# A fused recurrent-attention and MLP kernel: the opening fifth of its instruction order rewritten, with the first alpha and k loads in front of the first weight slice

## The chip, the cores and the metric

The kernel runs on one core of one Trainium2 chip. The core has five engines, each with its own queue of instructions that it works off strictly in order: PE (the matrix engine, with its weight loads shown apart as PEld), DVE (vector), ACT (scalar/activation), POOL (general purpose) and SP, which here only issues DMA transfers. Engines wait for each other through semaphores. Sixteen DMA engines move data between DRAM and the on-chip memory SBUF; matrix products land in a second memory, PSUM. The metric is the time of one execution in microseconds (us) on the device, as a median of several runs.

## The reference

Two blocks, one behind the other. The first is gated linear attention as a recurrence over 768 tokens, for 4 batches, 8 heads and head size 48, all in float32:

```
state = alpha[t][:, None] * state + outer(k[t], v[t])
y[t]  = q[t] @ state
```

The result, 3072 tokens by 384 features, goes into a two-layer MLP with hard-swish: `h = x @ w_in` (384 to 2048), `g = h * clip(h + 3, 0, 6) / 6`, `out = g @ w_out` (2048 to 384). The two weights come as float64 and are turned into float32 on the chip, by integer operations on their two 32-bit words.

## The kernel before, in words

**Tiling.** The sequence is cut into 24 chunks of 128 tokens (6 for each batch); two chunks make a group of 256 tokens for the MLP, so there are 12 groups. The recurrence of a chunk is done in a closed form: running products of alpha scale k and q, a masked product of the two gives the scores, and a 48x48 state is carried from chunk to chunk (in half chunks of 64 tokens). Groups 0 and 1 use the plain first product of the MLP (six matrix products for a pair of hidden blocks); from group 2 on it uses a scheme with fewer products and more sums, whose sums of weights (25 of them) and of activations DVE makes. The second product has a scheme of the same kind from group 1 on.

**The order of the work** is written out by hand as one list of about 1,790 words in one call of `run` (from line 753). Nothing rearranges it: each word calls one function of the table `steps` (line 730), which issues its instructions at once, and so each engine's queue holds its instructions in the order of the words. A word is the step's name, then its numbers: `la.1` is "load alpha of chunk 1", `f.0.6.3` "first product, group 0, part 6, into PSUM bank m3".

The steps that matter here, with their engines and lines:

- `la`, `lk`, `lq` (SP, line 256): alpha, k, q of one chunk, 192 KB in pieces of 192 bytes; `lv` (line 274): v, in two DMAs of 96 KB. `w` (lines 162, 166): one of 16 weight slices of 768 KB, eight of w_in, then eight of w_out.
- `d2`, `d1`, `dx` (ACT, lines 196, 186, 191), `d3` (DVE, lines 203 and 205, or 207, 208 and 210) and `d4` (POOL, line 217): the conversion of one weight slice. `d4` ends it, and frees the slice's load buffer.
- `ta`, `tk`, `tq` (PE, line 284): transposes into one of four PSUM banks t0 to t3; `ca` (ACT, line 302) copies alpha out. From chunk 6 on these are transposes on DVE (line 288).
- `r` (DVE, lines 311 and 315) and `p` (line 322): the running products; `k` and `q` (line 334): scaling k and q. `kb` (PE, line 376) and `ck` (ACT, line 380): k turned back.
- `u` (PE, line 431), `sm` (DVE, lines 439 and 441), `st` (POOL, line 411), `sv` (ACT, line 421, POOL, line 417): the state. `sc` (PE, line 348), `m` (DVE, line 358), `qa` (ACT, line 368), `ya`, `yb` (PE, line 457), `cy` (ACT, line 466): scores, mask, attention output, and its copy as the MLP's input.
- `fa`, `fb` (PE, line 491) and `f` (line 480): first MLP product by half groups and whole groups, into banks m0 to m3; `fr` (ACT, line 496) and `fg` (DVE, line 500): hard-swish. `b` (PE, line 518): second product of group 0. `P` (PE, line 705), `s`, `x`, `G` (DVE, lines 649, 666, 721): second product with sums. `M` (PE, line 602), `y`, `xc` (DVE, lines 539 to 543): first product with sums.
- `z.m.n` (PE, line 534): n products of the identity with itself, whose result nobody reads. There are 26 of them in the opening. One shows as two instructions in the profile. `pd` (POOL, line 251): six small memsets of the buffers for chunks 6 and up.

**What binds the loads.** All DMAs are issued by SP, in order, and their completion semaphores are used in turn, eight of them: the n-th DMA waits until the one eight before it has landed.

Of the kernel before, what the change touches and what calls it, by code (L numbers as in the profile page):

```python
# [17 lines left out]
def kernel(  # L18
# [42 lines left out]
    G = 2  # L61
# [512 lines left out]
    for i in range(8):  # L574
        r, o = divmod(i, 3)
        spots.append(raws[r].rearrange("p n w -> p (n w)").bitcast(FP)[:, o * QB : (o + 1) * QB])
    xc = consts.tile([C, len(X_SUMS), C], FP, tag="xc")
# [174 lines left out]
    with tc.manual_schedule():  # L752
        run("""z.0.5 z.0.3 z.0.1 qa.0.0 w.0 d2.0 d3.0 la.0 ta.0.0 z.0.8 lk.0 tk.0.1 la.1 ta.1.2
               lq.0 tq.0.3 lk.1 lv.0.0 d1.0 ca.0 r.0 p.0 k.0 kb.0.0 z.0.2 z.0.2 q.0 la.2 dx.0 ca.1
               r.1 ck.0 u.0.2.1 sm.0.0 qa.0.1 sv.0.1 tk.1.0 p.1 sc.0.2.3 w.2 lq.1 sm.0.1 k.1 m.0
               ta.2.0 z.0.2 d1.2 ca.2 d2.2 kb.1.0 ck.1 r.2 tq.1.2 q.1 dx.2 lv.1.1 u.1.3.1 z.0.3
               lq.2 w.1 lk.2 d4.0 lk.3 la.3 la.4 w.3 lq.3 lv.2.2 lk.4 w.5 pd.0 sv.0.0 pd.1 st.1
               sm.1.0 p.2 d3.2 sm.1.1 ya.0.3 yb.0 sc.1.0.2 m.1 d4.2 sv.1.1 cy.0 qa.1.1 sv.1.0 d1.1
               st.2 d2.1 dx.1 fa.0.1 tq.2.1 q.2 tk.2.3 k.2 fa.2.0 sc.2.0.2 d3.1 m.2 d4.1 ta.3.1
               ta.4.3 kb.2.0 qa.1.0 ca.3 r.3 ca.4 r.4 ya.1.2 yb.1 tk.3.1 fa.1.2 p.3 k.3 qa.2.1  # L760
               qa.2.0 cy.1 d2.3 d3.3 fb.2 fb.1 tq.3.1 q.3 sv.2.0 d1.3 ck.2 u.2.3.2 sm.2.0 d4.3
               fr.0.2.0 tk.4.0 d2.5 sv.2.1 k.4 sm.2.1 st.3 fg.0.2 d3.5 w.6 lv.3.0 lq.4 w.7 fb.0
               sc.3.1.3 m.3 kb.3.2 kb.4.0 f.0.3.3 ya.2.1 ck.3 d1.5 d4.5 d1.6 d2.6 d3.6 d4.6 sv.3.0
               qa.3.1 fr.0.1.0 fr.0.3.1 la.5 w.4 yb.2 u.3.3.2 sm.3.0 fg.0.3 fg.0.1 sm.3.1 f.0.5.0
               tq.4.3 f.0.6.3 ta.5.2 cy.2 ck.4 d2.7 qa.3.0 d1.7 d3.7 d4.7 fr.0.5.1 fr.0.0.0 sv.3.1
               fg.0.0 fg.0.5 p.4 d2.4 ya.3.0 yb.3 cy.3 fr.0.6.1 w.9 d2.9 ca.5 d1.9 d1.4 dx.4 la.6
               w.8 d3.4 lk.5 w.10 d3.9 ca.6 q.4 fg.0.6 d4.9 w.12 lq.5 lv.4.1 d2.8 f.0.7.2 st.4
               f.1.1.1 f.1.7.0 sc.4.0.2 f.1.3.3 qa.4.0 d1.8 fr.0.7.0 r.6 d3.8 d4.8 d4.4 w.11 fg.0.7
               m.4 fr.1.1.0 fr.1.7.1 fg.1.7 fg.1.1 d2.10 d1.10 f.1.0.2 d2.12 d3.10 r.5 d4.10 w.13
               fr.1.0.0 fr.1.3.1 fg.1.3 fg.1.0 d3.12 lq.6 f.1.6.0 f.1.2.1 u.4.1.0 tk.5.3 sm.4.0  # L770
               sv.4.0 d1.12 qa.4.1 d4.12 w.15 fa.4.3 fr.1.2.0 fr.1.6.1 d2.11 d2.13 f.1.4.2 d1.11
               sm.4.1 lv.5.0 lk.6 fg.1.2 k.5 kb.5.1 tq.5.3 d3.11 p.5 d4.11 tq.6 fg.1.6 q.5 p.6
               d3.13 d1.13 d4.13 tk.6 st.5 w.14 la.7 lk.7 ck.5 sv.4.1 b.0.0.1 ya.4.2 yb.4 sc.5.0.3
               m.5 cy.4 d2.15 fr.1.4.1 fg.1.4 d3.15 d2.14 d3.14 u.5.2 b.0.1 f.1.5.0 fb.4 b.1.0.2
               b.1.1 qa.5.0 fr.1.5.1 fg.1.5 d1.14 fr.0.4.0 d1.15 qa.5.1 d4.14 d4.15 sm.5.0 fg.0.4
               ca.7 sv.5.1 sv.5.0 ya.5.3 tk.7 s.1.0.0 x.0 k.6 x.1 y.6 y.1 yb.5 P.1.1.3 b.1.2 cy.5
               b.1.3 kb.6.0 P.1.0.0 b.0.2 lv.6.2 y.3 y.5 y.9 xc.2.1 y.2 s.1.1.1 y.7 s.1.3.2 x.2
               s.1.2.3 y.8 y.4 y.0 q.6 bo.1 K.1.0 G.1.0.0 P.1.2 K.1.1 s.1.4 xc.2.3 y.10 r.7 xc.2.4
               P.1.3.3 K.1.2 ck.6 P.1.4 b.0.3 xc.2.5 y.15 y.11 y.12 x.3 G.1.1.1 s.1.5 y.13 y.16 k.7
               P.1.5 u.6.3.0 sc.6.1.2 P.1.6 y.14 y.17 y.19 xc.2.6 sm.6.0 G.1.2.2 y.20 xc.2.0  # L780
               M.2.0.2 lv.12.1 la.8 O.1.1 O.1.0 ca.8 y.18 y.21 y.23 so.1 G.1.3.3 n.2.0.8 bo.0 lq.7
               lv.7.0 O.1.2 m.6 xc.2.2 xc.2.10 xc.2.7 tq.7 r.8 p.7 xc.2.8 sv.6.1 M.2.15.3 M.2.1
               kb.7.3 n.2.1.9 M.2.16 M.2.2 n.2.2.10 qa.6.1 M.2.7.0 n.2.7.11 sm.6.1 xc.2.9 q.7 p.8
               M.2.3 M.2.4 n.2.4.12 M.2.8 o.2.0.0 M.2.5 n.2.5.13 qa.7.0 st.7 sv.6.0 lk.8 O.1.3 lq.8
               lk.9 la.9 la.10 tk.8 tq.8 lq.10 lq.9 ya.6.1 yb.6 M.2.9 z.1.3 M.2.18.1 o.2.1.0
               e.2.1.1 M.2.10 cy.6 ck.7 sc.7.0.2 u.7.1.3 n.2.10.14 M.2.11 qa.7.1 ca.9 la.11 y.22
               M.2.6.2 h.2.1 q.8 m.7 e.2.0.0 h.2.0 n.2.11.15 qa.6.0 n.2.18.10 qa.8.1 M.2.12 M.2.19
               n.2.12.12 M.2.13 sm.7.0 sv.7.1 r.9 k.8 o.2.3.0 sv.7.0 ya.7.0 y.24 o.2.5.0 n.2.13.12
               o.2.2.0 yb.7 cy.7 sc.8.1.2 xc.3.1 o.2.2.1 e.2.2.1 xc.3.3 o.2.3.1 M.2.14 xc.3.4
               xc.3.0 xc.3.5 o.2.4.0 xc.3.7 xc.3.6 o.2.6.0 P.2.0.1 M.3.0.2 M.2.17 h.2.2 o.2.6.1  # L790
               e.2.3.0 h.2.3 o.2.7.0 K.2.0 n.3.0.12 M.3.1 n.3.1.9 e.2.5.1 M.3.7.0 n.3.7.13 xc.3.8
               o.2.7.1 xc.3.2 kt.8 e.2.6.0 h.2.6 tk.9 M.3.2 n.3.2.10 e.2.4.0 P.2.1.3 h.2.4 h.2.5
               s.2.0.14 e.2.7.0 G.2.0.1 h.2.7 M.3.3 M.3.4 n.3.4.8 k.9 s.2.1.11 M.3.8 o.3.0.0 ca.10
               kt.9 P.2.3.3 s.2.2.15 s.2.3.14 lv.8.2 kw.8 kr.8 lk.10 sm.7.1 xc.3.9 M.3.5 n.3.5.11
               K.2.2 e.3.0.1 xc.3.10 M.3.9 o.3.1.0 P.2.2 K.2.1 u.8.0.3 M.3.18.2 s.2.5 M.3.10
               n.3.10.14 n.3.18.15 e.3.1.0 s.2.4 P.2.4 tq.9 h.3.0 st.8 sv.8.0 M.3.11 n.3.11.8 tk.10
               p.9 sm.8.0 q.9 r.10 k.10 qa.9.0 qa.9.1 m.8 sm.8.1 h.3.1 M.3.19 o.3.5.0 kt.10 P.2.5
               G.2.2.0 st.9 M.3.12 sc.9.0.1 qa.8.0 n.3.12.10 o.3.3.0 kw.9 lv.9.0 kr.9 sv.8.1
               u.9.2.3 sm.9.0 sv.9.1 sv.9.0 G.2.1.2 sm.9.1 st.10 M.3.15.2 M.3.16 M.3.6.3 M.3.13 m.9
               o.3.4.0 o.3.6.0 tq.10 n.3.13.10 o.3.2.0 e.3.4.1 ya.8.2 yb.8 ya.9.3 yb.9 cy.9 M.3.14  # L800
               M.3.17 cy.8 xc.4.1 P.2.6 e.3.5.0 G.2.3.3 o.3.2.1 xc.4.3 h.3.4 xc.4.4 o.3.6.1 xc.4.5
               xc.4.0 xc.4.6 e.3.2.1 M.4.0.0 n.4.0.10 P.3.0.1 xc.4.7 o.3.7.0 p.10 h.3.5 o.3.3.1
               xc.4.8 M.4.7.3 M.4.1 xc.4.2 h.3.2 o.3.7.1 lk.11 O.2.2 tk.11 e.3.6.0 e.3.3.1 h.3.3
               P.3.1.2 e.3.7.1 n.4.1.13 M.4.2 K.3.0 ca.11 q.10 h.3.6 r.11 k.11 h.3.7 n.4.7.15
               lv.10.2 lv.11.0 kw.10 sc.10.0.1 kr.10 G.3.0.0 u.10.3.2 sm.10.0 qa.10.1 n.4.2.14
               M.4.3 M.4.4 M.4.8 s.3.0.9 xc.4.9 s.3.2.12 s.3.1.11 P.3.3.2 n.4.4.8 M.4.5 o.4.0.0
               e.4.0.0 sv.10.1 sm.10.1 xc.4.10 kt.11 O.2.0 O.2.3 lq.11 m.10 s.3.3.9 s.3.5 M.4.9
               o.4.1.0 P.3.2 sv.10.0 st.11 n.4.5.11 K.3.2 la.13 M.4.18.0 p.11 tq.11 lk.12 tk.12
               K.3.1 M.4.10 n.4.10.9 q.11 qa.10.0 n.4.18.12 e.4.1.1 la.12 s.3.4 ca.12 h.4.0 r.12
               P.3.5 G.3.2.1 h.4.1 M.4.11 P.3.4 n.4.11.8 M.4.12 n.4.12.14 qa.11.0 M.4.19 p.12  # L810
               G.3.1.3 lq.12 kw.11 O.2.1 tq.12 kr.11 u.11.3 sc.11.0.2 sv.11.0 O.3.1 lk.13 P.3.6
# [125 lines left out]
```

## Time and profile before

| | |
|---|---|
| median of 3 runs | 531.67 us (531.34 to 532.08) |
| the profiled execution's own time | 531.87 us |
| its span, first to last instruction | 530.1 us |
| PE busy | 520.6 us (98%) |
| DVE busy | 474.8 us (90%) |
| ACT busy | 257.5 us (49%) |
| POOL busy | 49.9 us (9%) |
| moved by DMA | 54.40 MB, of it 44.50 MB read from DRAM |

The profile comes from one execution. Its page gives the busy time of each engine, a picture of the span in 40 slices of 13.25 us, the chain of work that ended last, and groups of instructions by line. The trace behind it answers for any stretch: which instruction ran when, for how long, how long its engine sat idle before it and what released it; and, for a DMA, the time from its issue to its landing. Times in what follows count from the first instruction of the span. Consecutive instructions on an engine overlap a little, so a queue is added up by starts, not by durations.

### The profile page before, as it was taken

What the parts mean: (1) busy time and instruction counts of PE and PEld (TensorE: products, weight loads), DVE (VectorE), ACT (ScalarE), POOL (GpSimd) and SP (SyncE); (2) the same over time, 40 slices, a digit from 0 to 9 for tenths busy, and PEclk for the clock granted to TensorE, in tenths of its full rate; (3) what the DMA queues carried; (4) which work ended last, traced back from release to release, by engine and by line L of the source; (5) the groups of instructions that cost most, each with busy time, mean ns of one, the idle gap of its engine ahead of it and who ended that gap; (6) DMA issues with size and microseconds to landing.
All of it is one profiled execution on the core that took longest, in us unless ns stands there. A gap on an engine that the chain in (4) does not pass through costs nothing.

```text
span 530.1 us, 15131 instructions
## 1 busy us (share of the span) xinstructions
PE 520.6 (98%) x6306; PEld 495.8 (94%) x6306; DVE 474.8 (90%) x849; ACT 257.5 (49%) x503; POOL 49.9 (9%) x71
## 2 busy tenths in 40 slices
PE   7899999999999999999999999999999999999997
PEld 6688887789999999999999999999999999999997
DVE  7999999999999999998999999999999899595382
ACT  5789866003753644452644435642634544553340
POOL 7323343000000000000010000000000000000000
PEclk9999999999999999999999999999999999999999
DMA  9998877016515155254354456144464042100001
GB/s 171 218 251 247 246 208 171 1 37 157 123 29 124 29 125 125 59 138 104 81 112 112 96 122 139 24 116 106 112 142 102 16 92 56 44 2 2 15 16 37
DMA packets 124100, 54.40 MB, mean 103 GB/s; under 512 B 83328, under 2 KB 116864, under 8 KB 124032
## 3 DMA queue, kind: packets, MB, share of 16 engines
q1 hardware_dynamic: 124032, 53.44, 44.1%
q8 instruction: 49, 0.80, 0.7%
q14 instruction: 19, 0.16, 0.1%
HBM read 44.50 MB, written 8.91 MB: 101 GB/s over the span
## 4 chain that ended last, share of the span: by engine, by line
PE 92%; DMA 2%; DVE 2%; ACT 2%; POOL 0%; issue 0%; SPq 0%
PE m_ps L705 38%; PE m_ps L602 35%; PE m_ps L480 5%; PE t_ps L457 4%; PE m_ps L518 4%; PE t_ps L348 2%; PE t_ps L431 2%; DMA v<-in_v_dram 1%; DMA rings<-in_alpha_dram 1%; ACT raw L191 1%; DVE R L311 1%; PE m_ps L491 1%; PE t_ps L284 0%; POOL w L217 0%; PE m_ps L534 0%
## 5 line engine op out<-in xcount | busy, mean ns | idle before, releaser
L608 ACT COPY g_sb<-m_ps 128x512 f32<-128x512 f32 x110 | 63.5, 583 | 122.3 <-PE m_ps L602 101.7
L705 PE MATMUL m_ps<-w,g_sb 128*128 128x192 f32 x704 | 121.8, 327 | 0.0
L705 PEld LDWEIGHTS m_ps<-w,g_sb 128*128 128x128 f32 x704 | 113.7, 190 | 0.5
L705 PE MATMUL m_ps<-rings,g_sb 128*128 128x192 f32 x528 | 91.5, 326 | 0.0
L705 PEld LDWEIGHTS m_ps<-rings,g_sb 128*128 128x128 f32 x528 | 85.4, 190 | 0.4
L602 PE MATMUL m_ps<-xc,w 128*128 128x128 f32 x640 | 82.7, 277 | 0.0
L602 PEld LDWEIGHTS m_ps<-xc,w 128*128 128x128 f32 x640 | 77.5, 192 | 1.0
L496 ACT ACTIVATE r<-g_sb,half 128x512 f32<-128x512 f32 x80 | 56.8, 722 | 32.7 <-DVE g_sb L500 11.9
L500 DVE SCALAR_TENSOR_TENSOR g_sb<-r,g_sb 128x512 f32<-128x512 f32 x80 | 53.5, 680 | 4.5 <-ACT r L496 4.1
L602 PE MATMUL m_ps<-xT,raw 128*128 128x128 f32 x400 | 52.5, 277 | 0.0
L602 PEld LDWEIGHTS m_ps<-xT,raw 128*128 128x128 f32 x400 | 48.6, 192 | 0.6
L411 POOL TENSOR_TENSOR st<-sm,R 128x192 f32<-128x192 f32 x20 | 12.7, 635 | 340.6 <-DVE sm L441 293.8
L649 DVE TENSOR_TENSOR g_sb<-g_sb 128x512 f32<-128x512 f32 (+1 forms) x55 | 42.0, 792 | 0.2
L602 PE MATMUL m_ps<-xT,w 128*128 128x128 f32 x320 | 42.0, 276 | 0.0
L602 PEld LDWEIGHTS m_ps<-xT,w 128*128 128x128 f32 x320 | 39.3, 192 | 0.1
L368 ACT COPY A<-q 48x256 f32<-48x256 f32 x88 | 35.5, 403 | 5.1 <-DVE q L334 3.8
L358 DVE TENSOR_TENSOR A<-t_ps,mask 64x256 f32<-64x256 f32 x96 | 36.1, 414 | 0.4
L480 PE MATMUL m_ps<-xT,w 128*128 128x256 f32 x144 | 32.5, 381 | 0.0
L602 PE MATMUL m_ps<-xc,raw 128*128 128x128 f32 x240 | 31.8, 276 | 0.0
L311 DVE TENSOR_TENSOR_SCAN R<-t,ones 128x516 f32<-128x516 f32 x24 | 29.9, 1246 | 0.9 <-ACT t L302 0.8
L480 PEld LDWEIGHTS m_ps<-xT,w 128*128 128x128 f32 x144 | 26.9, 190 | 3.8
L602 PEld LDWEIGHTS m_ps<-xc,raw 128*128 128x128 f32 x240 | 29.6, 192 | 0.1
(104 smaller groups left out, 718.2 us busy)
## 6 DMA issues: line engine op xcount, KB each, us to landing
raw<-in_moe_w_out_dram SPq DMA_DIRECT2D x8, 768.0 KB, 5.1
raw<-in_moe_w_in_dram SPq DMA_DIRECT2D x6, 768.0 KB, 6.7
v<-in_v_dram SPq DMA_DIRECT2D x48, 96.0 KB, 3.2
out_dram<-oh SPq DMA_DIRECT2D x44, 96.0 KB, 1.7
far<-kq SPq DMA_DIRECT2D x64, 64.0 KB, 2.2
kb<-far SPq DMA_DIRECT2D x64, 64.0 KB, 2.1
aq<-in_alpha_dram SPq DMA_DIRECT2D x36, 96.0 KB, 2.5
qq<-in_q_dram SPq DMA_DIRECT2D x36, 96.0 KB, 2.6
```

Of the source, the lines that this page charges most:

```text
L311: nc.vector.tensor_tensor_scan(out=reverse(R, n - 1, n), data0=reverse(ax, n, n), data1=reverse(ones, n, n), initial=0.0, op0=ALU.mult, op ...
L358: nc.vector.tensor_tensor(out=to[:, a], in0=sc[a][half], in1=mask[half, half].unsqueeze(1).to_broadcast([HB, NP, HB]), op=ALU.mult)
L368: nc.scalar.copy(out=to[:, a], in_=Q_t[j][64 * a : 64 * a + D, :, half])
L457: nc.tensor.matmul(y_of(j, (i + 1) // 2, p)[:, HB * b : HB * b + HB], vb[:, p, e : e + 32], A_t[j][:, b, 2 * p + a], start=(b == 0 and i = ...
L480: nc.tensor.matmul(h[:, f], w1[:, kk, o : o + C], xT_t[g][:, kk], start=(kk == 0), stop=(kk == KT - 1))
L496: nc.scalar.activation(out=to, in_=h, func=AF.Relu, bias=half, scale=1.0 / 6.0)
L500: nc.vector.scalar_tensor_tensor(out=to, in0=r, scalar=1.0, in1=h, op0=ALU.min, op1=ALU.mult)
L518: nc.tensor.matmul(o_t[c], gs[0][:, f, c * C : (c + 1) * C], w2[:, f], start=(f == 0), stop=(f == NF - 1))
L602: nc.tensor.matmul(acc[g][i][:, f * C : (f + 1) * C], spots[w][:, f * C : (f + 1) * C], x_of(g, x), start=(first and f == 0), stop=last, s ...
L608: nc.scalar.copy(out=slots[z], in_=acc[g][i])
L649: nc.vector.tensor_tensor(out=out, in0=in0, in1=in1, op=ALU.subtract)
L705: nc.tensor.matmul(to[g], a, rhs[:, f], start=(first and f == 0), stop=(last and f == HF - 1), skip_group_check=True)
```

## The change

The same 1,790 words, in another order. They differ up to word 435; from there to the end the two lists are identical. By the profile's clock that is about the first 135 us. No step is added, removed or altered.

- SP: w slice 0 was the first transfer, in front of alpha 0, k 0, alpha 1, q 0, k 1. Now alpha 0, k 0, alpha 1 go first, then w slice 0, then k 1, q 0. Further on, v 1 moves in front of q 1; the loads of chunks 3 and 4 and slice 3 go as a3, w3, v2, a4, k4, k3, q3 (before: k3, a3, a4, w3, q3, v2, k4).
- DVE: `d3.0` goes from the front of the queue to behind `r.1`; `p` behind `k` for chunk 0; `q.1` from in front of `sm.1.0` to behind `sm.1.1`. Further on most `r`, `p`, `q`, `fg` and `d3` change places with neighbours.
- ACT: `d2.0` and `d1.0` go behind the copies of alpha 0 and 1.
- PE: alpha 0, k 0, alpha 1 are transposed right behind each other; eight of the idle products stand behind these three; two stand in front of `u.0`, and the two behind `ta.2` are gone from there. `ta.4` stands behind `yb.1`, `fb.1` behind `kb.3`, chunk 3's attention in front of chunk 2's, `sc.4` in front of `f.0.7`, `P.1.0` in front of `P.1.1`.
- POOL: `pd.0` and `pd.1` go from behind `d4.0` to behind `d4.7` and `d4.8`.
- Behind `xc.2.0`: `tk.7`, `ca.7`, `r.7`, `k.7` and `y.14` go from in front of `M.2.0` to behind it.

```
-        run("""z.0.5 z.0.3 z.0.1 qa.0.0 w.0 d2.0 d3.0 la.0 ta.0.0 z.0.8 lk.0 tk.0.1 la.1 ta.1.2
-               lq.0 tq.0.3 lk.1 lv.0.0 d1.0 ca.0 r.0 p.0 k.0 kb.0.0 z.0.2 z.0.2 q.0 la.2 dx.0 ca.1
-               r.1 ck.0 u.0.2.1 sm.0.0 qa.0.1 sv.0.1 tk.1.0 p.1 sc.0.2.3 w.2 lq.1 sm.0.1 k.1 m.0
-               ta.2.0 z.0.2 d1.2 ca.2 d2.2 kb.1.0 ck.1 r.2 tq.1.2 q.1 dx.2 lv.1.1 u.1.3.1 z.0.3
-               lq.2 w.1 lk.2 d4.0 lk.3 la.3 la.4 w.3 lq.3 lv.2.2 lk.4 w.5 pd.0 sv.0.0 pd.1 st.1
-               sm.1.0 p.2 d3.2 sm.1.1 ya.0.3 yb.0 sc.1.0.2 m.1 d4.2 sv.1.1 cy.0 qa.1.1 sv.1.0 d1.1
-               st.2 d2.1 dx.1 fa.0.1 tq.2.1 q.2 tk.2.3 k.2 fa.2.0 sc.2.0.2 d3.1 m.2 d4.1 ta.3.1
-               ta.4.3 kb.2.0 qa.1.0 ca.3 r.3 ca.4 r.4 ya.1.2 yb.1 tk.3.1 fa.1.2 p.3 k.3 qa.2.1
...
-               P.1.5 u.6.3.0 sc.6.1.2 P.1.6 y.14 y.17 y.19 xc.2.6 sm.6.0 G.1.2.2 y.20 xc.2.0
-               M.2.0.2 lv.12.1 la.8 O.1.1 O.1.0 ca.8 y.18 y.21 y.23 so.1 G.1.3.3 n.2.0.8 bo.0 lq.7
-               lv.7.0 O.1.2 m.6 xc.2.2 xc.2.10 xc.2.7 tq.7 r.8 p.7 xc.2.8 sv.6.1 M.2.15.3 M.2.1
...
+        run("""z.0.5 z.0.3 qa.0.0 la.0 z.0.1 ta.0.0 lk.0 la.1 w.0 tk.0.1 ta.1.2 z.0.8 lk.1 lq.0
+               ca.0 r.0 z.0.2 ca.1 d2.0 k.0 p.0 r.1 d3.0 kb.0.0 z.0.2 tq.0.3 q.0 ck.0 d1.0 dx.0
+               tk.1.0 p.1 lv.0.0 la.2 qa.0.1 w.2 z.0.2 u.0.2.1 sm.0.0 sv.0.1 k.1 sc.0.2.3 sm.0.1
+               m.0 ta.2.0 ca.2 d1.2 r.2 kb.1.0 ck.1 d2.2 lv.1.1 lq.1 u.1.3.1 z.0.3 tq.1.2 lq.2 w.1
+               lk.2 la.3 w.3 lv.2.2 la.4 lk.4 lk.3 lq.3 d4.0 w.5 sv.0.0 st.1 sm.1.0 d3.2 sm.1.1 q.1
+               p.2 ya.0.3 yb.0 sc.1.0.2 m.1 tq.2.1 q.2 dx.2 sv.1.0 cy.0 st.2 d4.2 sv.1.1 d1.1 d2.1
+               dx.1 qa.1.0 fa.0.1 tk.2.3 k.2 d3.1 d4.1 ta.3.1 sc.2.0.2 fa.2.0 m.2 kb.2.0 ca.3
+               qa.1.1 r.3 ya.1.2 yb.1 ta.4.3 fa.1.2 d2.3 d3.3 d1.3 cy.1 fb.2 ca.4 ck.2 qa.2.0
+               sv.2.0 r.4 d4.3 qa.2.1 fr.0.2.0 d2.5 w.6 lv.3.0 lq.4 w.7 u.2.3.2 tk.3.1 fb.0 sm.2.0
+               k.3 p.3 tq.3.1 tk.4.0 sm.2.1 st.3 fg.0.2 q.3 d3.5 f.0.3.3 sc.3.1.3 kb.3.2 fb.1 m.3
...
+               fr.0.5.1 ta.5.2 f.0.6.3 ya.3.0 yb.3 ya.2.1 yb.2 w.9 la.6 w.8 p.4 d3.7 d4.7 pd.0
+               fg.0.5 lk.5 w.10 q.4 fg.0.1 ca.5 d2.4 cy.3 fr.0.6.1 cy.2 d2.9 d1.4 d1.9 fr.0.0.0
+               d3.4 d3.9 fg.0.0 sc.4.0.2 f.0.7.2 f.1.7.0 f.1.1.1 dx.4 fr.0.7.0 d2.8 st.4 d4.9 w.12
...
+               y.17 y.12 y.19 x.3 y.20 G.1.1.1 xc.2.6 P.1.6 G.1.2.2 xc.2.0 tk.7 M.2.0.2 O.1.1 O.1.0
+               ca.8 ca.7 y.18 y.21 sm.6.0 r.7 y.23 so.1 G.1.3.3 n.2.0.8 bo.0 lq.7 lv.7.0 O.1.2 m.6
+               xc.2.2 k.7 xc.2.10 xc.2.7 tq.7 y.14 r.8 p.7 xc.2.8 sv.6.1 M.2.15.3 M.2.1 kb.7.3
```

## The prediction, made before the changed kernel was run

> **What bounds the kernel now.** I read the page first (busy shares, the 40 slices):
>
> ```profile
> PE 520.6 (98%) x6306; PEld 495.8 (94%) x6306; DVE 474.8 (90%) x849; ACT 257.5 (49%) x503; POOL 49.9 (9%) x71
> PE   7899999999999999999999999999999999999997
> DVE  7999999999999999998999999999999899595382
> ...
> ```
>
> PE is the bound, and only its first slices have holes. The table by stretches sizes them (after the length: busy time of PE, PEld, DVE, ACT, POOL):
>
> ```profile
> 0.00:13.25 13.25, 9.66 (x70) 8.89 (x74) 9.54 (x18) 6.92 (x9) 9.38 (x24) 1.00 1.13 171
> 13.25:26.50 13.25, 10.71 (x247) 9.23 (x247) 12.21 (x25) 10.11 (x18) 4.62 (x13) 1.00 1.06 218
> 26.50:39.75 13.25, 12.98 (x246) 11.89 (x246) 12.68 (x21) 11.20 (x20) 3.83 (x3) 1.00 1.08 251
> 39.75:53.00 13.25, 12.96 (x212) 11.03 (x211) 12.46 (x21) 13.02 (x24) 4.39 (x3) 1.00 0.87 247
> 53.00:132.00 79.00, 79.00 (x690) 65.89 (x689) 76.97 (x126) 36.04 (x63) 15.98 (x11) 1.00 0.53 136
> 132.00:530.00 398.00, 395.24 (x4857) 388.92 (x4855) 350.94 (x643) 180.18 (x373) 11.69 (x18) 1.00 0.35 80
> ```
>
> PE idles 3.59 + 2.54 + 0.27 + 0.29 = 6.7 us before 53 us, nothing from there to 132, and 2.8 behind that, where the word list is unchanged. PE's work is the same before and after, the 26 idle products included, so **the time changes by the change in PE's idle time up to 135 us**. From 53 to 132 DVE too is busy for 97%. What PE waits for, from the list of its waits up to 45 us (total, times, longest):
>
> ```profile
> PE m_ps L534 <- POOL ident masks.py:199: 1.5, 1, 1.5
> PE t_ps L284 <- DMA rings<-in_alpha_dram: 1.3, 1, 1.3
> PE t_ps L284 <- DVE k L334: 1.3, 1, 1.3
> PE t_ps L376 <- ACT t L302: 0.8, 1, 0.8
> PE t_ps L376 <- DVE k L334: 0.5, 1, 0.5
> ```
>
> The 1.5 stays: every engine starts with it. The next is alpha 0; the rest comes through DVE's chain. The timeline of the start (start, duration, idle before and its end in brackets):
>
> ```profile
> 1.46 4.18 PE L534 MATMUL m_ps<-ident 128*128 128x128 f32 x18 [1.46 <-POOL ident masks.py:199]
> 5.67 0.91 ACT L196 ACTIVATE w<-raw 128x768 f32<-128x768 f32 x1 [3.65 <-DMA raw<-in_moe_w_in_dram]
> 6.61 0.93 DVE L203 TENSOR_SCALAR w<-w 128x768 f32<-128x768 f32 x1 [2.43 <-ACT w L196]
> 6.96 0.63 PE L284 MATMUL t_ps<-ident,rings 128*128 128x128 f32 x4 [1.31 <-DMA rings<-in_alpha_dram]
> 7.42 1.95 PE L534 MATMUL m_ps<-ident 128*128 128x128 f32 x16
> 7.57 0.69 DVE L205 TENSOR_SCALAR w<-w 128x768 uint32<-128x768 uint32 x1
> 8.24 1.23 DVE L311 TENSOR_TENSOR_SCAN R<-t,ones 128x516 f32<-128x516 f32 x1
> 16.05 1.52 DVE L358 TENSOR_TENSOR A<-t_ps,mask 64x256 f32<-64x256 f32 x4
> 18.03 1.23 DVE L311 TENSOR_TENSOR_SCAN R<-t,ones 128x516 f32<-128x516 f32 x1 [0.47 <-ACT t L302]
> ```
>
> Two things matter. Nine idle products (18 instructions) hold PE until 5.64, so alpha is no use earlier. And DVE does `d3.0` from 6.61 to 8.24, while alpha 0 is still on its way: before, this work cost the chain nothing.
>
> **Loads.** Before, the landings were: w0 5.65, alpha 0 6.82, k 0 8.03, then one load of 192 KB each 1.2 us (q 0 10.44, k 1 11.65). With three loads in front, w0 lands near 5.65 + 3 x 1.2 = 9.25. Its 768 KB take about 2.1 us at the 386 GB/s of the best early stretch, so alpha 0, k 0, alpha 1 land near 4.7, 5.9, 7.1, q 0 at 11.65, k 1 at 10.4; the eighth DMA ends as before. Bounds for alpha 0: 4.4 (w0's landing less one load) and 6.8 (no gain). I take 4.7, the row it is nearest to being w0 in that place. The other moved transfers keep bytes and pace: v 1 comes about 1.2 earlier (it goes past q 1), q 1 as much later, slice 3 about 2.5 earlier, k 3 from 25 to near 32, where `tk.3` now stands at 33.7.
>
> **DVE's chain**, by starts. `ta.0` 5.66 instead of 6.96 and `ca.0` behind it (8.24 - 6.96 = 1.28 from transpose to `r.0`): `r.0` 6.95, **a gain of 1.29**. Then `r.0` 1.46, `k.0` 0.6, `p.0` 1.15, `r.1` 1.46 bring DVE to 11.6, and now `d3.0` stands there: 1.39 by the same pair at 22.00 (0.93 + 0.69 in the rows above, beside POOL's memsets). Its inputs are there: w0 9.25, `d2.0` 0.91 on ACT. So **the gain is spent again**: `q.0` 13.0, `p.1` 13.6 (0.3 slower, since `d4.0` now runs on POOL beside it, as `r.1` took 1.63 instead of 1.23 beside POOL), `sm.0.0` 15.05, `k.1` 15.6, `m.0` 16.2 against 16.05.
>
> What follows gains a little. `dx.0` and `qa.0.1` fill ACT before alpha 2's copy is due, so `ca.2` runs at 16.4 instead of 17.43 and the wait of 0.47 in front of `r.2` goes: `r.2` 17.7 (18.03). `u.1` has v 1 and `ck.1` at 18.5 (19.43 and 19.91), and `sm.1.0` no longer waits 0.38. Then `d3.2`, `sm.1.1`, `q.1` 21.15, `p.2`, `m.1` 22.9 (23.57), `q.2`, `k.2`, `d3.1` 25.6 (26.32), `m.2` 26.95 (27.73). DVE is 0.8 ahead; by `d3.6`, whose predecessors are then the same set, about 1.2 (44.2 against 45.4).
>
> **PE's idle time** on that chain: 1.46 at the start; 0.4 between k 0 and alpha 1; 0.8 before `tq.0` (q 0 is later); 1.2 before `ta.2` (it takes the bank from `k.1`; before 1.26); 0.6 before `kb.1` (0.77); 1.0 before `u.1`, since the two idle products behind `ta.2` moved forward; 0.3 each before `sc.1` and `sc.2`; 0.55 before `kb.2` (m.2's bank; 0.27). Sum 6.6. Before, up to there: 6.4, and 0.3 at 42.66. At the end of `yb.1` PE is at 29.75 against 30.65, with one transpose (`ta.4`, 0.55) less done: 0.35 ahead; if `ya.2`'s 0.29 at 42.66 goes too, **0.64 ahead**. Some of it I give back: `ta.4` arrives as alpha 4 lands (near 29.8).
>
> **From 40 to 135 us** PE can only keep or lose this. I added up DVE's and PE's words in both orders, from the times of before. Then `u.3` behind `m.3`, `kb.4` behind `k.4`, `sc.4` behind `q.4` and `f.0.7` behind `fg.0.1` come 0.2 to 0.4 too early for DVE (before, slacks of 0.7 to 4.4), which DVE's lead of 1.2 covers over PE's lead of 0.6. Later the least slacks are 0.6 (`P.1.5` behind `s.1.5`; before 1.0) and about 0.4 (`kb.7` behind `k.7`, now behind `y.23`; before over 5), while `M.2.0` gains 5 us of slack from the 4.7 us of DVE work put behind it. So 0.2 of waits, bounded by 0 and 1. POOL's memsets (12 x 0.33) leave 12.6 to 15.4, where DVE is slowed beside them, for a stretch in which POOL is idle for over 70%: nothing. `d4.0` to 15.5 is hidden: `fa.0` needs it at 23. ACT's table load moves with its first instruction, 1.28 in an idle 3.65: nothing.
>
> **Sum**: -0.64 + 0.2 = -0.4 on an execution of 531.87 (span 530.1, 1.8 around it), which lies 0.2 above its median of 531.67: **531.3 us**, a change too small to tell from none (I call 0.2%, 1.06 us, the limit of that).
>
> **Rivals.** (1) *Within 0.2%*, as above: chance 0.38, its own range 530.6 to 532.7.
> (2) *Slower: alpha 0 comes late.* Small pieces open the queue, and the first transfer starts on a cold DMA path; no row shows alpha in that place. Every 0.1 us behind 5.6 delays `r.0` by 0.1, and `d3.0` still stands on the chain. At the bound 6.8 DVE is 1.2 later all along: PE +1.2 - 0.4, and the four tight places of 40 to 52 lose their cover (+0.4): +1.2, 532.9. It decides from about 6.5 on, or with as much delay at w0 (past 10.7, `d3.0` waits). The rows speak for the arithmetic, the pace of 1.2 against so late a landing. With the tight places failing for another reason, 0.24.
> (3) *Slower: PE's clock falls back.* The first 18 instructions took 4.18/18 = 232 ns each, the next 16 1.95/16 = 122, all at a granted clock shown as 1.00. In the new order PE does only eight transposes between 14.7 and 18.5, 3.8 us; before, the longest such stretch was 9.4 to 12.1. If PE dropped to the slow rate for another 4.2 us there, `u.1` to `sc.1` (0.57 + 0.75 + 0.6 + 1.1 + 0.7 = 3.7) would double, less 0.6 of idle time: +3.1 - 0.4, 534.4; half of that if it recovers sooner. Chance 0.06. The Trainium skill says in "TensorE: Matmul & The Clock Gate", Part 1, that an idle window of about 3.4 us halves the clock, and in Part 4 that transposes don't count as busy; by these the stretch could just hold such a window. This trace has the slow start (232 ns) but no such fall.
> (4) *Faster by over 0.2%.* PE still waits 5 us between 6 and 29 in my chain. If `p.1` isn't slowed beside POOL (0.3), `d3.0` costs the least a half slice shows (1.36), transfers land 0.5 earlier with the shorter queue in front (0.8 before `tq.0`, 0.4 before `ta.1`), and the later waits vanish: -0.4 - 0.3 - 0.5 - 0.2 = -1.4, 530.3. Chance 0.32.
>
> The range goes to 529.4 below (all the waits of (4) half gone) and 533.6 above (half of (3), all of (2)). Faster 0.32, same 0.38, slower 0.30.
>
> **What would show it.** Right: alpha 0's transposes at 5.7, `r.0` near 7.0, `d3.0` between 11 and 13.5, `m.0` within 0.4 of 16.05, PE's idle time up to 53 us of 6 to 6.8, none from 53 to 132. Wrong: PE waiting for DVE past 40 us (lines 348, 376, 480), alpha 0 landing past 5.7, idle products or `u.1` at double duration near 19 us, or idle time below 5.6.

## The result: slower by 0.4%, and by how long the clock stayed low

The changed kernel takes 534.45 us in the median of 22 executions (531.06 to 536.43), the kernel before beside it 531.64 us (531.26 to 534.09): a ratio of 1.0041, 95% interval 1.0025 to 1.0057. The prediction was 531.3 us, range 529.4 to 533.6; the median lies 0.85 us above that range.

The 22 times do not lie around one value, and without this they can't be understood: executions of one kernel differ in the TensorE clock that was granted. In three the mean clock was 1.00, and they took 531.11 to 531.13 us. In three it was 0.997: 531.06 to 531.21. In the other sixteen it was 0.990 to 0.994, and these took 533.24 to 536.43. So the forecast sum came true where the clock held (531.12, some 0.5 us under the kernel before), and in most executions something else was paid on top: 2 to 5 us.

The profile of the changed kernel shows an execution whose clock held (531.11 us). Its page, busy shares and the first rows of the 40 slices:

```profile
PE 519.5 (98%) x6306; PEld 495.7 (94%) x6306; DVE 475.2 (90%) x849; ACT 258.1 (49%) x503; POOL 52.7 (10%) x71
PE   7799999999999999999999999999999999999997
...
PEclk9999999999999999999999999999999999999999
```

Its table by stretches (length, then busy time of PE, PEld, DVE, ACT, POOL, and the granted clock):

```profile
0.00:13.25 13.25, 10.58 (x102) 9.94 (x102) 9.65 (x20) 6.99 (x8) 6.64 (x20) 1.00 1.05 188
13.25:26.50 13.25, 9.86 (x240) 8.41 (x241) 12.73 (x25) 11.78 (x19) 6.78 (x5) 1.00 1.16 249
26.50:39.75 13.25, 12.92 (x209) 11.57 (x209) 12.85 (x22) 10.53 (x21) 4.80 (x4) 1.00 0.95 207
39.75:53.00 13.25, 12.63 (x248) 11.12 (x248) 12.49 (x21) 13.09 (x24) 6.00 (x10) 1.00 0.95 284
53.00:132.00 79.00, 79.00 (x665) 66.47 (x664) 77.28 (x126) 35.76 (x63) 18.18 (x18) 1.00 0.50 129
```

PE's idle time is 2.67 + 3.39 + 0.33 + 0.62 = 7.0 us up to 53 us, and none from there to 132. Before, it was 6.7, and 7.1 in a second profile of the kernel before (before_again, below), so the sum has hardly moved. But it lies elsewhere: the first stretch lost 0.9 of it, the second gained 0.85. What PE waits for there, by the list of its waits up to 30 us (total, times, longest):

```profile
PE m_ps L534 <- POOL ident masks.py:199: 1.5, 1, 1.5
PE t_ps L348 <- DVE s L439: 1.5, 1, 1.5
PE t_ps L284 <- DMA rings<-in_q_dram: 0.9, 1, 0.9
PE t_ps L431 <- ACT kb L380: 0.8, 1, 0.8
PE t_ps L376 <- ACT t L302: 0.7, 1, 0.7
```

The wait for alpha 0 (1.3) and that for `k.1` in front of `ta.2` (1.3) have gone. New is the second line: `sc.0` waits for DVE's copy in `sm.0.0`. The timeline of that place, first before the change, then after it:

```profile
13.13 0.57 PE L431 MATMUL t_ps<-v,kb 64*48 64x48 f32 x32
13.64 0.66 PE L284 MATMUL t_ps<-ident,rings 128*128 128x128 f32 x4
13.81 0.33 DVE L439 COPY s<-t_ps 128x192 f32<-128x192 f32 x1
14.06 1.22 DVE L322 TENSOR_TENSOR_SCAN P<-t 128x516 f32<-128x516 f32 x1
14.22 0.69 PE L348 MATMUL t_ps<-q,k 48*64 48x64 f32 x32
```

```profile
12.40 0.57 PE L431 MATMUL t_ps<-v,kb 64*48 64x48 f32 x32
...
12.91 1.23 DVE L322 TENSOR_TENSOR_SCAN P<-t 128x516 f32<-128x516 f32 x1
...
13.06 2.72 POOL L217 TENSOR_TENSOR w<-w,raw 128x768 int32<-128x768 int32 x1 [6.05 <-ACT raw L191]
14.06 0.33 DVE L439 COPY s<-t_ps 128x192 f32<-128x192 f32 x1
...
14.44 0.69 PE L348 MATMUL t_ps<-q,k 48*64 48x64 f32 x32 [1.47 <-DVE s L439]
```

`u.0` (L431) and `sc.0` (L348) both use bank t2 (`u.0.2.1`, `sc.0.2.3`), so the scores can't start before DVE has copied the state out of it. The change put `p.1` (L322) in front of that copy on DVE; before, it stood behind, and PE had the transposes of `tk.1` (L284, at 13.64) to do in the meantime, so `sc.0` followed without a wait. Beside it POOL's `d4.0` (L217) starts only 0.15 us after `p.1`.

### The profile page after: what moved, and what is told of

It is laid out like the page before. It is cut to its first block, busy times and chain, and to the rows that moved or that the text cites. A ratio compares the mean times of both kernels' runs of the same rounds, so it can differ in the third digit from the quotient of the medians.

```text
span 529.3 us, 15133 instructions
## 1 busy us (share of the span) xinstructions
PE 519.5 (98%) x6306; PEld 495.7 (94%) x6306; DVE 475.2 (90%) x849; ACT 258.1 (49%) x503; POOL 52.7 (10%) x71
## 4 chain that ended last, share of the span: by engine, by line
PE 93%; DVE 3%; DMA 2%; SPq 1%; ACT 1%; issue 0%; POOL 0%; ACTq 0%; POOLq 0%; DVEq 0%
PE m_ps L705 38%; PE m_ps L602 35%; PE m_ps L480 5%; PE t_ps L457 4%; PE m_ps L518 4%; PE t_ps L348 2%; PE t_ps L431 2%; DMA raw<-in_moe_w_in_dram 2%; PE m_ps L534 1%; SPq L256 1%; DVE P L322 1%; PE t_ps L284 1%; PE m_ps L491 1%; DVE R L311 0%; DVE q L334 0%
## 5 line engine op out<-in xcount | busy, mean ns | idle before, releaser
L411 POOL TENSOR_TENSOR st<-sm,R 128x192 f32<-128x192 f32 x20 | 13.8, 690 | 348.1 <-DVE sm L441 296.8
L322 DVE TENSOR_TENSOR_SCAN P<-t 128x516 f32<-128x516 f32 x24 | 29.6, 1232 | 0.2
```

The lines of the kernel that those rows point to most:

```text
L322: nc.vector.tensor_tensor_scan(out=P_t[j], data0=aX[j % 2][:, 0:n], data1=ini[j % 2], initial=0.0, op0=ALU.mult, op1=ALU.add)
```

## The experiments

**again: the changed kernel, unchanged.** It was run again for a profile of an execution whose clock falls.

> The changed kernel itself once more, for the spread and for the profile of an execution in which the granted clock is below 1.00 (16 of 22 executions had 0.994 or less). Clock theory: the long executions (533 to 536.4) have PE instructions at double duration in one stretch that begins between 13 and 23 us, where PE does little but transposes; 0.994 is two windows of about 3.4 us at half rate, 0.990 is three; outside that stretch PE's idle time is as in the 531.1 execution. Rival (waits): the long executions have idle time of PE past 40 us, behind DVE or a late load, of 2 to 5 us, and the low clock is only its companion.

Median 535.42 us (530.73 to 536.07), ratio 1.0048 (1.0027 to 1.0070); nine of ten executions at a clock of 0.997 or less. The profile taken is that of 536.07 us. Its table, cut at the moments at which the granted clock changes (6.25, 16.49 and 26.73) and into parts of 3.41 us between (columns as above):

```profile
6.25:9.67 3.42, 3.42 (x33) 3.42 (x32) 2.52 (x4) 2.10 (x3) 0.75 (x1) 1.00 1.28 266
9.67:13.08 3.41, 2.82 (x52) 2.38 (x49) 3.34 (x6) 3.01 (x3) 0.00 (x0) 1.00 1.27 188
13.08:16.49 3.41, 0.00 (x0) 0.00 (x0) 3.38 (x3) 1.13 (x3) 2.34 (x2) 1.00 1.28 266
16.49:19.91 3.42, 2.52 (x38) 2.01 (x39) 2.91 (x8) 1.66 (x4) 0.51 (x1) 0.50 1.21 264
19.91:23.32 3.41, 2.69 (x41) 2.23 (x40) 1.97 (x4) 3.15 (x4) 0.00 (x0) 0.50 1.06 158
23.32:26.73 3.41, 3.41 (x79) 2.91 (x82) 2.93 (x5) 1.36 (x4) 1.96 (x2) 0.50 1.08 281
```

The third row is a window in which PE did nothing; from its end on the clock is 0.50 for three windows. The timeline of this execution shows why it did nothing, and what half the clock does to PE:

```profile
12.40 0.57 PE L431 MATMUL t_ps<-v,kb 64*48 64x48 f32 x32
...
13.49 1.82 POOL L217 TENSOR_TENSOR w<-w,raw 128x768 int32<-128x768 int32 x1 [6.49 <-ACT raw L191]
13.54 2.86 DVE L322 TENSOR_TENSOR_SCAN P<-t 128x516 f32<-128x516 f32 x1
...
16.33 0.33 DVE L439 COPY s<-t_ps 128x192 f32<-128x192 f32 x1
...
16.71 1.13 PE L348 MATMUL t_ps<-q,k 48*64 48x64 f32 x32 [3.74 <-DVE s L439]
```

Here `d4.0` starts 0.05 us ahead of `p.1`, and `p.1` takes 2.86 us instead of 1.23. `sc.0` waits 3.74 us instead of 1.47, and takes 1.13 instead of 0.69; from there to `ya.0` PE runs at this slow rate. Such a drop of the granted clock from 1.00 to 0.50 is called a fall from here on. Over the whole execution PE is busy 523.5 us here against 519.5 in the one whose clock held, for the same instructions, and idle 10.8 against 9.8: of the 5.0 us between the two, 4.0 are slower work. From 40 to 132 us PE waits for nothing, so the rival (waits past 40 us) is out.

**z_back and before_no_z: the idle products' place.** The two idle products that the change moved from behind `ta.2` to in front of `u.0` go back; and in the kernel before, the same two are left out (nobody reads their result).

```
z_back       - ... w.2 z.0.2 u.0.2.1 ... m.0 ta.2.0 ca.2 ...
             + ... w.2 u.0.2.1 ... m.0 ta.2.0 z.0.2 ca.2 ...
before_no_z  - ... ta.2.0 z.0.2 d1.2 ...
             + ... ta.2.0 d1.2 ...
```

> The changed kernel with one thing undone: the two idle products stand again behind the transposes of alpha 2 instead of in front of u.0. Clock theory: most executions keep the clock, about 531.0 (0.5 to 0.6 under the kernel before) with at most a few long ones. Rival (waits): nothing changes, long and short executions in the same share, median 533 to 535.

> The kernel before with the two idle products behind the transposes of alpha 2 left out; from 14.9 to 19.4 us PE then does eight transposes and waits. Nothing else is changed and the output does not depend on them. Clock theory: long executions (533 to 536) appear in the kernel before too, in a good share; the others stay at 531.6. Rival (waits): 531.6 as before, for the products stand where PE waits.

z_back: 534.03 us (530.24 to 536.15), 1.0032 (1.0008 to 1.0055), ten of twelve at 0.997 or less. So their place alone is not the cause. before_no_z: 531.59, 0.9999 (0.9987 to 1.0012), three of twelve, against four of 35 of the kernel before beside it: not the good share that I expected, and too few to tell whether the loss of half a microsecond of PE work there matters.

**z_more: more of them.** Nine idle products more in the changed kernel: three each behind `u.0`, `ta.2` and `kb.1`.

```
-  u.0.2.1 sm.0.0 ...         m.0 ta.2.0 ca.2 d1.2 r.2 kb.1.0 ck.1
+  u.0.2.1 z.0.3 sm.0.0 ...   m.0 ta.2.0 z.0.3 ca.2 d1.2 r.2 kb.1.0 z.0.3 ck.1
```

> The changed kernel with nine idle products more, three each behind u.0, behind the transposes of alpha 2 and behind kb.1, in places where PE waits 1.5, 0.7 and 0.8 us anyway (three take 0.73 us). Clock theory: no long executions at all, 531.0 to 531.3. Rival (waits): long executions as often as in the changed kernel, and 0 to 0.5 us more for the added products.

531.12 us (530.53 to 534.94), 0.9998 (0.9979 to 1.0016); two of twelve below 0.998. More PE work in the stretch, fewer falls, and the end of it no later: the added work lies in waits. In the profile of 534.94 us `d4.0` (13.18) was ahead of `p.1` (13.26, 2.85 us) again.

**d1_first, no_d4, p1_mid: the collision on DVE.** Is it `d4.0` beside `p.1` that brings the falls? d1_first lets `d4.0` start earlier, no_d4 leaves it out, p1_mid puts `p.1` later.

```
d1_first  - ... q.0 ck.0 d1.0 dx.0 ...      + ... q.0 d1.0 ck.0 dx.0 ...
no_d4     - ... lk.3 lq.3 d4.0 w.5 ...      + ... lk.3 lq.3 w.5 ...
p1_mid    - ... tk.1.0 p.1 lv.0.0 ...       + ... tk.1.0 lv.0.0 ...
          - ... u.0.2.1 sm.0.0 sv.0.1 ...   + ... u.0.2.1 sm.0.0 p.1 sv.0.1 ...
```

> The changed kernel with one ACT word earlier: `d1.0` (0.9 us) in front of `ck.0` instead of behind it, so that `dx.0` ends and POOL's `d4.0` starts about 0.2 us earlier, now always ahead of DVE's scan `p.1`. PE's and DVE's orders are unchanged. Theory of the collision (a POOL operation that started first holds the scan up for its whole length): `p.1` takes 2.8 us in the profile, sc.0 waits for 3.5 us or more, PE does under 1.7 us of work in whatever window of 3.41 us lies there, so the clock falls in all runs: median 535 to 536.5, no run at 531. Rival (the falls come from PE's order alone, the collision is only beside it): the same mixture as the changed kernel, six in ten or so at 533 to 536 and the rest at 531.

> The changed kernel with POOL's `d4.0` left out (the low bits of the first weight slice are not added, so the first projection uses a coarser slice; DVE, ACT and PE keep every instruction). Theory of the collision: `p.1` takes 1.23 us in every run, the wait in front of sc.0 never exceeds about 1.5 us, so PE's least work in a window of 3.41 us is 1.46 (worked out on the profiled execution whose clock held), which lies under 1.7 for only about a quarter of the places a window can lie at: falls in 2 to 4 runs of 12, median near 531.2. Rival (the 1.5 us wait is enough by itself): falls in eight runs or more, median 533 to 535.

> The changed kernel with p.1 directly behind sm.0.0's copy (start 13.9 to 14.3 instead of 12.9), so that POOL's `d4.0` (starts 13.1 to 13.5, 1.83 us alone) has always started first. If the one that starts first keeps the other out for its whole length, p.1 lasts until d4.0's end plus 1.2 us: 13.1 + 1.83 + 1.2 = 16.1, that is 2.0 to 2.3 us for p.1, and d4.0 stays at 1.83. If both only share a path, p.1 takes 1.5 or so and d4.0 over 2.2. m.0 is later by the same 0.8 to 1.1 us.

no_d4: 534.50 us (533.07 to 535.28, five executions), 1.0054 (1.0042 to 1.0066), all five at 0.990 to 0.996, and `p.1` took 1.23. My theory gave two to four of twelve: the rival stands. The wait of 1.5 us (1.48 in this profile) is enough without the collision, and for long falls too: two of the five stand at 0.990. d1_first (535.05 us, 1.0049 (1.0030 to 1.0069), ten of twelve) and p1_mid (533.90 and 535.50 us, 1.0055 (1.0037 to 1.0072), both with a fall) did not do what they were made for: in both profiles `p.1` still started first. p1_mid, in its two executions, still tells that `p.1` behind `sm.0.0`, as before the change, is no cure either: the wait in front of `sc.0` shrank to 0.46 us, that in front of `ta.2` grew to 1.03. And they show the other side of the collision. In p1_mid:

```profile
13.89 1.22 DVE L322 TENSOR_TENSOR_SCAN P<-t 128x516 f32<-128x516 f32 x1
...
14.08 2.67 POOL L217 TENSOR_TENSOR w<-w,raw 128x768 int32<-128x768 int32 x1 [7.07 <-ACT raw L191]
```

Whichever of the two started first kept its time (1.23 or 1.83 us), and the other took until then plus its own (2.67 to 2.84 for `d4.0` in five profiles, 2.85 to 2.90 for `p.1` in three). The Trainium skill says in "SBUF — State Buffer", under "Who interferes with whom", that a DVE instruction with two SBUF inputs and a GpSimd instruction that reads SBUF shut each other out for a whole instruction, by who issues first; these profiles agree.

**p1_late, full, full_tr: the stretch filled.** p1_late moves `p.1` behind `m.0`, so that `sm.0.0` no longer waits for it. full adds nine idle products to that, where PE then waits; full_tr has fifteen transposes of the identity in their place.

```
p1_late  - ... tk.1.0 p.1 lv.0.0 ... m.0 ta.2.0 ...
         + ... tk.1.0 lv.0.0 ... m.0 p.1 ta.2.0 ...
full     - u.0.2.1 sm.0.0 ...        p.1 ta.2.0 ca.2 d1.2 r.2 kb.1.0 ck.1
         + u.0.2.1 z.0.1 sm.0.0 ...  p.1 ta.2.0 z.0.3 ca.2 d1.2 r.2 kb.1.0 z.0.5 ck.1
full_tr  + u.0.2.1 zt.2 sm.0.0 ...   p.1 ta.2.0 zt.5 ca.2 d1.2 r.2 kb.1.0 zt.8 ck.1
         + def idle_t(n):
         +     for _ in range(n):
         +         nc.tensor.transpose(bank_m[0][:, 0:C], ident, ident)
         - "z": idle,
         + "z": idle, "zt": idle_t,
```

> The changed kernel with the DVE scan `p.1` moved from in front of `sm.0.0` to behind `m.0` (its result is first read by `q.1`). Same work everywhere. sm.0.0's copy follows `u.0` at once, so sc.0 starts near 13.4 instead of 14.44, and `d4.0` has ended before `p.1` starts (15.6), so no collision. PE's idle time does not go, it moves behind ta.2 and kb.1, in front of `u.1`, which waits for v of chunk 1 (lands 16.8 to 17.2): 0.6 and 1.2 us. Theory (a fall needs a window of 3.41 us with under about 1.8 us of PE work): the leanest window lies at 14.7 to 18.1 with some 1.3 us, so falls stay in a third to a half of the runs, with one or two windows at half clock; median 531 to 533.5. Rival (only the waits in front of sc.0 matter): no falls, median 530.8 to 531.1.

> The order of p.1 behind `m.0` as in the run beside it, and nine idle products more where PE then waits: one behind `u.0`, three behind ta.2, five behind kb.1 (18 instructions, 2.2 us). Theory: every window of 3.41 us from 5 us on holds over 2.2 us of PE work, so no run falls: all twelve at 530.6 to 531.3, median 531.0, ratio 0.998 to 0.9995. Rival (the clock falls for another reason than too little PE work): the same share of falls as without the nine products. If the products themselves delay the chain, the runs with the clock held lie above 531.3.

> The run `full` with its nine added idle products replaced by fifteen transposes of the identity (two behind `u.0`, five behind ta.2, eight behind kb.1; a transpose took about 0.15 us, a product 0.24). Theory (any work of PE counts; windows with 1.91 us of transposes out of 2.19 us kept the clock in the kernel before): no falls, all runs 530.6 to 531.4, median 531.0. Rival (transposes do not count as busy, as the Trainium skill has it in "TensorE: Matmul & The Clock Gate", Part 4): falls at least as often as with p.1 behind `m.0` alone (7 of 12), rather more, since the waits are then filled with work that does not count: median 531.1 to 534.

p1_late: 531.08 us (530.61 to 533.85), 0.9999 (0.9987 to 1.0011). Seven of twelve are at 0.997 or less, but only two at 0.994: the falls are shorter, not gone. full: **530.94 us (530.53 to 532.23), 0.9990 (0.9982 to 0.9999), none of eleven with a fall**. It is 0.1% faster than the kernel before, hardly more than the measurement can tell. full_tr: 531.35 us (530.91 to 533.53), 0.9994 (0.9984 to 1.0004), none of eleven with a fall either; what its longest execution paid at a mean clock of 1.00 is not shown. The table of the profile of full, from the rise of its clock in windows of 3.41 us:

```profile
7.34:10.76 3.42, 3.42 (x33) 3.42 (x31) 3.38 (x5) 1.70 (x3) 0.00 (x0) 1.00 1.41 195
10.76:14.17 3.41, 2.88 (x64) 2.40 (x67) 3.34 (x7) 3.37 (x5) 0.14 (x1) 1.00 1.20 262
14.17:17.58 3.41, 3.40 (x57) 3.03 (x48) 3.36 (x8) 3.36 (x7) 3.27 (x3) 1.00 1.41 201
17.58:21.00 3.42, 3.11 (x107) 2.54 (x106) 3.32 (x6) 3.06 (x5) 0.24 (x1) 1.00 1.13 292
```

PE is busy nearly throughout. So p1_late against full, seven of twelve against none of eleven with nothing but 2.2 us of useless work between them, shows that too little PE work is what makes the clock fall; and full_tr, that transposes count as work. The Trainium skill has the latter the other way in "TensorE: Matmul & The Clock Gate", Part 4; here, with float32, by the runs, they kept the clock.

**w_first, tk1_back, opening_back, before_d3, before_again: which part of the change?** The first weight slice first again; `tk.1` back behind `u.0`; load, `d2.0` and `d3.0` of the opening back (PE's order in it stays as changed); and in the kernel before only DVE's `d3.0` moved behind `r.1`. before_again is the kernel before, for a second profile.

```
w_first       - qa.0.0 la.0 ... lk.0 la.1 w.0 tk.0.1     + qa.0.0 w.0 la.0 ... lk.0 la.1 tk.0.1
tk1_back      - tk.1.0 p.1 ... u.0.2.1 sm.0.0 sv.0.1     + p.1 ... u.0.2.1 sm.0.0 sv.0.1 tk.1.0
opening_back  w_first, and  - ca.1 d2.0 k.0 p.0 r.1 d3.0   + ca.1 k.0 p.0 r.1
                            - w.0 la.0                     + w.0 d2.0 d3.0 la.0
before_d3     - w.0 d2.0 d3.0 la.0 ... ca.1 r.1 ck.0     + w.0 d2.0 la.0 ... ca.1 r.1 d3.0 ck.0
```

> The changed kernel with the first weight slice's load in front of alpha, k and alpha again, as before the change; every other order stays as changed. alpha 0 lands near 6.8 instead of 3.67 (the kernel before), `r.0` starts near 8.2 instead of 6.5 and `d3.0` still stands behind r.1, so DVE's chain is 1.5 us late throughout. Theory A (the lean stretch of PE comes from the orders of DVE and PE, not from the loads): the stretch between `u.0` and u.1 is as lean as in the changed kernel, so falls stay in over half of the runs; with the clock held 531.8 to 532.6, median 533 to 536. Theory B (earlier alpha is what moved PE's early work apart from the rest): falls in at most two runs of 12, median 531.8 to 532.6.

> The changed kernel with the transposes of k of chunk 1 (`tk.1`, 0.6 us) back behind `u.0`, so that they lie in the wait for sm.0.0's copy. u.0 starts up to 0.5 us sooner, the wait in front of sc.0 shrinks from 1.5 to about 1.3, the sum of PE's work in a window hardly changes. Theory (a window with under about 1.93 us of PE work drops the clock, wherever its holes are): falls as often as in the changed kernel, at least half of the runs, median 532.5 to 535.5. Rival (the single long wait counts): falls become rare, median 531.1.

> The changed kernel with the opening as before the change: the first weight slice is loaded first, ACT's `d2.0` and DVE's `d3.0` (1.3 us) run while alpha 0 is still on its way; everything behind `r.0` keeps the changed orders (tk.1 in front of `u.0`, the idle products moved forward, and so on). Theory (the lean stretch of PE comes from `d3.0`, which now stands between r.1 and q.0 on DVE and holds PE up where it has little work): falls become as rare as in the kernel before, at most two runs of 12, median 531.2 to 532. Rival (the later orders make the stretch lean, whatever the opening): falls in half of the runs or more, median 533 or above.

> The kernel before with one DVE word moved, `d3.0` from in front of `r.0` to behind r.1; loads and all other orders as before the change. DVE's chain is 1.3 us later from `sm.0.0` on (m.0 near 17.4 instead of 16.05). Theory (d3.0's place makes PE's stretch lean): falls in half of the runs or more; with the clock held 532.5 to 533, median 533 to 536. Rival (other orders of the change are needed for it): falls in at most two runs of 12, median 532.3 to 533.

> The kernel before, unchanged, for a second profile of it: 531 to 532.5, clock held, m.0 near 16, and PE's work in the windows of 3.41 us that the granted clock marks never under 1.93 us.

| run | median us | ratio (95%) | clock 0.997 or less |
|---|---|---|---|
| w_first | 534.57 | 1.0056 (1.0037 to 1.0074) | 6 of 6 |
| tk1_back | 533.49 | 1.0031 (1.0010 to 1.0053) | 9 of 12 |
| opening_back | 533.59 | 1.0043 (1.0030 to 1.0057) | 6 of 6 |
| before_d3 | 535.03 | 1.0069 (1.0056 to 1.0082) | 5 of 5 |
| before_again | 531.93 | one execution | no |

The kernel before, in the four sets of executions beside all these runs, was at 0.997 or less in 9 of 98. before_d3 shows that moving `d3.0` alone is enough to make it fall; in its profile `d4.0` (15.02) is ahead of `p.1` (15.05, 2.90 us), and `ta.2` waits 2.96 us. opening_back shows that moving it back is not enough to cure the changed kernel, against my theory: the orders that stay changed, PE's in the opening among them, suffice. No single part is the cause.

Part of the price in some of these runs is not the fall. The clock starts low: the first 18 instructions of the kernel before took 232 ns each, the next 16 took 122. In the profiles of w_first, opening_back and before_no_z it rises only at 10.6 to 10.9 us, against 4.5 to 7.4 in the other thirteen that recorded it; the first twelve transposes of w_first take 3.50 us, those of the changed kernel 1.69. The mean clock does not count this stretch, so an execution at 0.997 can be slower there than in the changed kernel. In w_first the window from 3.77 to 7.18 held 2.04 us of PE work and was not followed by the rise; what makes the rise late was not tested.

**The windows, all profiles together.** In each profile that recorded the clock I cut the first 130 us, from the clock's rise on, into windows of 3.413 us, the length of which every fall is a multiple (3.41, 6.83 or 10.24 us), and took PE's busy time in each from the table by stretches. The twelve falls each begin at the end of a window with little PE work:

| profile | PE busy in the window before the fall, of 3.41 us |
|---|---|
| again, before_d3, before_no_z | 0.00, 0.53, 1.37 |
| no_d4, z_back, z_more, p1_mid | 1.55, 1.68, 1.70, 1.71 |
| d1_first (two falls), opening_back | 1.90 and 1.76, 1.78 |
| p1_late, w_first | 1.94, 1.95 |

No window with 1.97 us or more was followed by a fall. Four with less were not: 1.93 and 1.94 (the changed kernel's first profile), 1.81 (no_d4) and 1.75 (before_again, for which I had expected none under 1.93). So the edge lies near 1.95 us, 57% of a window, with a little blur. The Trainium skill has such a window in "TensorE: Matmul & The Clock Gate", Part 1, with this length, and says that it runs freely, which these profiles bear out; it asks for an idle window, and here one that was more than half busy was enough.

Since the windows don't start with the kernel, what counts is the least PE work for any place of the window. The same tables, for windows of 3.41 us that start at:

| start, us | 11.2 | 12.0 | 12.8 | 13.6 | 14.4 | 15.2 | 16.0 |
|---|---|---|---|---|---|---|---|
| before (first profile) | 2.93 | 2.92 | 2.15 | 2.15 | 1.62 | 1.66 | 2.20 |
| before_again | 2.94 | 2.96 | 2.16 | 2.14 | 1.86 | 2.09 | 2.45 |
| changed, clock held | 1.94 | 1.94 | 1.46 | 1.89 | 1.94 | 1.93 | 2.20 |
| p1_late | 2.60 | 2.88 | 2.27 | 1.94 | 1.81 | 1.74 | 2.40 |
| full | 2.88 | 2.88 | 2.88 | 3.11 | 3.40 | 3.40 | 3.23 |

The profile of p1_late is one whose clock fell at 17.35, so its windows from 14.4 on hold some work at half the clock. The changed kernel is at or under the edge for starts over more than 4 us, longer than a window: wherever the windows lie, one of them hits the lean stretch, and only the blur lets it pass. In the kernel before the lean part is about 1 us wide, and in the second profile hardly there. That agrees with 19 of 22 against 9 of 98, though I can't work the shares out from it: the table of before would let one expect more than one in ten.

## Why the prediction was wrong

- **"The time changes by the change in PE's idle time"**: this bold step failed, and with it the premise in front of it, that PE's work is the same before and after. Neither holds when the clock changes. The sum of idle time was nearly right (6.6 forecast, 7.0 measured, 6.7 before), but when 1.5 us of it or more lie within one window of 3.41 us they can take the clock: in `again` the same instructions kept PE busy 4.0 us longer.
- **Rival (3), the clock falls back, with a chance of 0.06**: right in kind, wrong in chance and place. That its time, 534.4, is nearly the median of 534.45 is luck: it doubled 3.7 us of work inside 4.2 us of slow rate, where only 2.1 us of work would fit, and the median is one place in a mixture of falls of 6.83 us (533.2 to 534.8) and of 10.24 us (535.2 to 536.4). I judged it by a window without any counted work, for which only the stretch of 14.7 to 18.5 with its eight transposes would do. But transposes count, and the bar is 57% of a window, not zero. By that bar the forecast itself was a warning: 0.8 idle before `tq.0`, 1.2 before `ta.2`, 0.6 before `kb.1` and 1.0 before `u.1` lie between about 11 and 19 us.
- **"1.2 before `ta.2`"**: failed. The long wait stands one word earlier, in front of `sc.0`: 1.5 us for bank t2. Before, `sm.0.0`'s copy stood ahead of `p.1`, and `tk.1` lay between `u.0` and `sc.0`, so the shared bank cost nothing. I followed DVE's chain to `m.0` and took PE to follow it.
- **"`p.1` 13.6 (0.3 slower, since `d4.0` now runs on POOL beside it)"**: mis-sized, both ways: 0 where `p.1` starts first, 1.63 where `d4.0` does (2.86 against 1.23), with 0.05 us between the two starts in one profile.
- **The loads**: alpha 0 landed at 3.91 us, not 4.7, w0 at 8.41, not 9.25 (3.67 in the expectation for w_first is 0.24 too early): the small pieces moved sooner than w0's place in the queue had shown. Rival (2), alpha 0 late, fell. `r.0` was at 6.48 (6.95 forecast) for another reason: alpha 0 was there in time, and the idle products in front of its transposes ended at 5.22 instead of 5.64, since the clock rose at 4.94 instead of 5.49.
- **"The gain is spent again" on `d3.0`**: right in part. It ran from 10.89 to 12.20, and of the 1.76 us gained at `r.0` (8.24 to 6.48) 0.79 was left at `m.0` (16.05 to 15.26; 16.2 forecast).
- **The sum, -0.4 on 531.87**: right in number in the executions whose clock held, 531.11 to 531.13, but by luck. By its own rule the forecast's idle sums (6.6 against 6.4 + 0.3) give -0.1, not the -0.64 that was read off the two chains. In the profile PE reaches the unchanged words about 0.7 us earlier with 0.3 us more idle time: the same 6306 instructions kept it busy 519.5 us instead of 520.6, 0.3 of that in the shorter slow start and the rest spread over several lines of the opening. No wait of PE showed between 53 and 132 us, as forecast.

What stays open: which of the change's words make the stretch lean. Each that was tried alone left the falls; and why the kernel before falls as seldom as it does.

## What to carry to other kernels

Ask of a reordering not only how long TensorE idles but where: lay windows of 3.4 us over its first stretches, at every offset, and compare the least busy time with about 2 us. Where it is under that, put work there that nobody needs, transposes or products alike, into waits that exist anyway; that was worth more here (z_more's median lies 3.3 us under the changed kernel's) than the order itself (0.5 us where the clock held). And read a median of mixed executions as a mixture: the sum over a profile with a full clock tells the price of the order, the share of falls tells the rest.

## What the hardware did that I had not expected

- The clock falls after a window with up to 1.95 us of PE work out of 3.41, and stays at half for one to three windows in the profiles (0.987, in one execution of w_first, makes four in all). In the 32 executions of the changed kernel a mean clock of 0.997 (one window) cost nothing to 0.8 us, 0.993 or 0.994 (two) 2 to 4, 0.990 (three) 4 to 5.3.
- After a fall it came back only behind windows with over 3 us of PE work at half clock (3.27 to 3.42 in eleven profiles); 2.92 and 3.09 were not enough. At the start of d1_first it rose behind 3.00, so this edge has a blur too.
- The order of two instructions on DVE and POOL that start 0.05 us apart decides over 1.6 us: the first shuts the other out.
- The kernel before had this fall too, in about one execution of eleven (9 of 98).
